# The first channel layer of two more batches by seven block products, and 134 shifted entries in a planned instruction order

## The chip, the cores and the metric

The kernel runs on one core of one Trainium2 chip. The metric is the device time of that core in microseconds (us). Before the change it is 276.57 us, the median of three runs (276.26 to 276.59). The profile comes from one further execution, which took 276.21 us. The engines are named as in the profile: PE is the matrix engine, PEld its weight load, DVE the vector engine, ACT the scalar engine, POOL and SP the two that mostly issue transfers. A "pass" is one matmul instruction: it streams its moving columns past 128x128 loaded weights.

## The reference

Eight batches go through windowed attention with a linear bias, and the result through two mixing layers:

```python
# attention: B=8, H=8 heads, S=576 positions, D=64
scores = scale * q @ k.T ; scores = where(0 <= i-j < 128, scores - slope[h]*|i-j|, -1e9)
x = (softmax(scores) @ v) with the heads side by side        # 8 x 576 x 512
# mixer
h  = relu(x.T @ w_tok1) @ w_tok2                              # 576 -> 256 -> 576, along positions
u  = x + h.T
h2 = relu(u @ w_ch1) @ w_ch2                                  # 512 -> 1536 -> 512, along channels
out = u + h2
```

Inputs and output are float32. The kernel works in bf16 with float32 sums.

## The kernel before

**Batches and stages.** Batches are numbered from 0, so the fourth and the sixth are 3 and 5. Each has four blocks of 128 positions; two batches share one more block for the 64 positions left over of each (the "tail" block). A batch passes through `side` (attention scores L770 and L816, exponentials on ACT L785, masks on DVE L795, values L858, reciprocals L871 and normalisation L874 or, on ACT, L880; then the token mix L905, L915, and L948, L944, whose sums with x go to `ub` by DVE L966), and then through `main`. `main` of batch b is written together with `side` of batch b+1, so the two share the engines. Between them, for batches 3 to 7, `ub` is turned into `uT` by transfers that SP issues (L974, one for each block); SP also issues the turns of q and k (L722) and most stores of the output.

**First channel layer.** `main` computes relu(u @ w_ch1) into `r2`: 12 chunks of 128 hidden rows for 512 positions. A plain chunk (`chunk`, L1460) is four passes of 512 columns into one PSUM bank, and one relu, on ACT (L1466) or DVE (L1467). The tail block has its own passes (L1503, L1548).

**Seven products.** `unit` replaces four chunks. It regards hidden rows, channels and positions as halved, and forms the 2x2 block product from seven block products instead of eight, each of four passes of 256 columns (L1360). They need the differences of the halves of `uT` (`halves`, L1323: four DVE subtractions a batch, stored in `tt`) and of the weights (`WS`, made once at L688). Three banks y, z, w are used: products 1, 6, 7 and 4 add up in y, product 2 is in z, products 5 and 3 in w. Three intermediate sums are copied out as e1, e5, e2 (`keep`, L1375, ACT or DVE, into the five float32 buffers `raw`/`ob` that also hold outputs). Three sums are completed on DVE (`join`, L1384: bank plus copy, to bf16), each followed by a relu in place (L1386 on DVE or L1388 on ACT); the fourth quarter is relued straight from y (L1411, ACT). Product 6 waits for the copy of 1, product 7 for the copy of 6, product 4 for the join of 7. They are declared in the order of `UORDER`, 1, 5, 2, 6, 3, 7, 4. The list `UNITS` says for each batch how many of its three groups of four chunks go this way; before, only the last batch has any.

**Second channel layer.** It already takes seven products in all batches (`second`, L1637, 84 passes of 256 columns), with DVE sums of `r2` (L1485) ahead of it and DVE additions behind it (L1608).

**Who sets the order.** The order of every engine's instructions is computed while the program is built. `Plan.op` records each operation with its engine, a cost in ns, a rank, a not-before (`after`), its predecessors and its buffers; `Plan.run` plays the operations through these costs and picks, for each engine, the candidate that could start first, the lower rank among those that are equal. An operation with `other` may go to either DVE or ACT. PSUM banks and other buffers are handed out in the same pass. The outcome is a fixed program: each engine takes its instructions strictly in the order written, and waits where an operand or a buffer is not ready. Units may use all eight banks only once the last score operation of the batch beside them is placed (`gated`); until then they have four, as the value products and the token mix have.

Of the kernel before, what the change touches and what calls it, by code (L numbers as in the profile page):

```python
# [71 lines left out]
class Plan:  # L72
# [59 lines left out]

    def run(self):
        ops = self.ops
        dice = [random.Random(x) for x in SEEDS]
        for o in ops:
            if SEEDS[o.part]:
# [241 lines left out]
GROUPS = (((0, 1, 2, 3), 250),)  # L379
UORDER = (1, 5, 2, 6, 3, 7, 4)  # L380
UNIT_RANK = 0
UNIT_LATE = False
SECOND_LATE = False
GATE = True
BANKS = 8
ALIKE = 0
UNITS = [0, 0, 0, 0, 0, 0, 0, 3]
FILL = 60000.0
START = 4300.0
LATE = (1500.0, 2790.0)  # L390
# [26 lines left out]
def kernel(  # L417
# [244 lines left out]
    def weight_sums():  # L662
        lo, hi = slice(0, HN), slice(HN, DM)
        for g in range(2):
            a, z = slice(3 * g, 3 * g + 3), slice(HK + 3 * g, HK + 3 * g + 3)
            got = []
            for i, x, y in ((0, WC2[:, a, hi], WC2[:, a, lo]), (1, WC2[:, z, hi], WT[:, 0, a, :]),
                            (2, WC2[:, z, hi], WC2[:, a, hi]), (3, WC2[:, z, lo], WT[:, 1, a, :])):
                def go(i=i, x=x, y=y, a=a):
                    dve_.tensor_tensor(out=WT[:, i, a, :], in0=x, in1=y, op=ALU.subtract)  # L670
                needs = [lc2[3 * g]] if i == 0 else [lc2[3 * g], lc2[HK + 3 * g]] + ([got[i // 2]] if i % 2 else [])
                got.append(plan.op("DVE", 154 + 3 * HN / 1.92, go, RANKT + i, needs=needs))
            lt.append(got)
# [3 lines left out]
    def hidden_sums():  # L677
        for u in range(NHT // 4):
            up, dn = slice(2 * u * P, 2 * (u + 1) * P), slice(DCH // 2 + 2 * u * P, DCH // 2 + 2 * (u + 1) * P)
            x, y = slice(0, NCB // 2), slice(NCB // 2, NCB)  # L680
            own = slice(2 * u * P, 2 * (u + 1) * P)
            got = []
            for i, f, a, z in ((0, ALU.add, WC1[:, x, dn], WC1[:, y, dn]),
                               (1, ALU.subtract, WS[:, 0, :, own], WC1[:, x, up]),
                               (3, ALU.subtract, WC1[:, y, up], WS[:, 1, :, own]),
                               (2, ALU.subtract, WC1[:, x, up], WC1[:, x, dn])):
                def go(i=i, f=f, a=a, z=z, own=own):
                    dve_.tensor_tensor(out=WS[:, i, :, own], in0=a, in1=z, op=f)  # L688
                needs = [lc1[x] for x in (2 * u, 2 * u + 1, 6 + 2 * u, 7 + 2 * u)]
                needs += [got[-1]] if i in (1, 3) else []  # L690
                got.append(plan.op("DVE", 154 + 2 * 2 * P / 1.92, go, RANKS + i, needs=needs, after=SUMS_AT))
            ls.append({1: got[0], 2: got[1], 4: got[2], 3: got[3]})
# [12 lines left out]
    weight_sums()  # L705
    if any(UNITS):
        hidden_sums()
# [621 lines left out]
    def unit(b, u, rank, uT, tt, r2):  # L1329
# [24 lines left out]
        def product(m, bk, more=(), new=True):  # L1354
            l, r, ws, ts = L[m]

            def go():
                for c in range(2):
                    for cb in range(2):
# [6 lines left out]
                         **({"makes": bk} if new else {"adds": bk}))  # L1366
            if UNIT_LATE and new:
                marks["wait"].append(op)
            return rk

        def half_of(x):
            return x().rearrange("p (c n) -> p c n", c=2)

        def keep(e, bk, rk):
            return plan.op("ACT", 600, lambda: act_.copy(out=e()[:, :], in_=bk()[:, :]), rk + UNIT_RANK, makes=e, uses=[bk],  # L1375
                           other=("DVE", 690, lambda: dve_.tensor_copy(out=e()[:, :], in_=bk()[:, :])))

        def mark(op, rows):
            for t in range(rows.start, rows.stop):
                r2.parts.setdefault(t, []).append(op)  # L1380

        def join(e, bk, rows, cols, rk):
            o = lambda: r2()[:, rows, cols]
            add = plan.op("DVE", 690, lambda: dve_.tensor_tensor(out=o(), in0=half_of(bk), in1=half_of(e), op=ALU.add),  # L1384
                          rk + UNIT_RANK, uses=[bk, e], part=(r2, ("sum", rows.start, cols.start)))
            mark(plan.op("DVE", RELU, lambda: dve_.tensor_scalar(out=o(), in0=o(), scalar1=0.0, scalar2=None, op0=ALU.max),  # L1386
# [47 lines left out]
    def main(b, rank):  # L1434
# [76 lines left out]

        if not UNITS[b]:
            turn_ = [0, 1, 2, 6, 7, 8, 3, 4, 5, 9, 10, 11] if quick else list(range(NHT))
# [6 lines left out]
        else:  # L1520
            tt = halves(b, rank, uT)
            for u in range(NHT // 4):
                if u >= NHT // 4 - UNITS[b]:
                    rk = unit(b, u, rank, uT, tt, r2)
# [205 lines left out]
```

## Time and profile before

| what | value |
|---|---|
| median of three runs | 276.57 us |
| profiled execution | 276.21 us |
| its span, first to last instruction | 274.2 us |
| PE busy | 267.9 us (98%) |
| DVE busy | 209.4 us (76%) |
| ACT busy | 136.9 us (50%) |
| granted PE clock | 1.000 |

The time of the execution is 2.0 us longer than the span of its instructions. Batch 3's first layer starts at 121.1 us of the span and its last channel pass ends near 156.1; for batch 5 these are 183.5 and 218.5; the units of the last batch run from 245 to 261 us. A matmul's listed duration (273 or 379 ns) holds its time in the pipeline; what a pass costs in a row of passes is read from the chain of work, as the time of a piece over its count.

### The profile page before, as it was taken

To read this page: it belongs to the slowest core of one execution; us is meant where nothing else is said; L and a number is where in the kernel's file an instruction comes from. 1 tells how busy PE (TensorE), PEld (TensorE's weight loads), DVE (VectorE), ACT (ScalarE), POOL (GpSimd) and SP (SyncE) were. 2 spreads that over 40 slices of the span, in tenths; PEclk is the share of its full clock that TensorE was granted. 3 is DMA by queue.
4 is the path that set the end of the run, shared out by engine and by line. 5 is a ranking of instruction groups with operands and counts; after the bars stand their busy time and mean duration, and the time that the engine had idled before them with its cause. 6 is when DMAs were issued, how large, how long until landed. Compare 5 with 4: busy or idle time off the path is not lost.

```text
span 274.2 us, 7149 instructions
## 1 busy us (share of the span) xinstructions
PE 267.9 (98%) x2896; PEld 182.2 (66%) x2896; DVE 209.4 (76%) x482; ACT 136.9 (50%) x221; POOL 114.3 (42%) x146
## 2 busy tenths in 40 slices
PE   8989999999999999999999999999999999999994
PEld 5767566676686656585658656486658655489983
DVE  7987699977997479675968469684969469697972
ACT  6963795326871396207930097206940087205500
POOL 8979796830496009600890009700850410022000
PEclk9999999999999999999999999999999999999999
DMA  8999999999999999979999939989995810143014
GB/s 201 178 175 181 166 159 182 155 157 197 157 118 141 199 161 103 154 119 199 192 151 136 211 127 89 150 119 214 181 142 91 229 42 2 28 108 116 2 41 151
DMA packets 160336, 38.57 MB, mean 141 GB/s; under 512 B 146544, under 2 KB 159472, under 8 KB 160304
## 3 DMA queue, kind: packets, MB, share of 16 engines
q0 software_dynamic: 109968, 19.64, 90.2%
q1 hardware_dynamic: 49104, 17.70, 34.3%
q10 hardware_dynamic: 1232, 0.79, 1.0%
q8 instruction: 22, 0.36, 0.6%
q14 instruction: 10, 0.08, 0.1%
HBM read 35.85 MB, written 9.44 MB: 165 GB/s over the span
## 4 chain that ended last, share of the span: by engine, by line
PE 92%; DMA 4%; ACT 1%; issue 1%; POOL 0%; DVE 0%; POOLq 0%
PE ps L1637 27%; PE ps L1460 26%; PE ps L858 6%; PE ps L770 5%; PE ps L905 4%; PE ps L948 4%; PE ps L1503 4%; PE ps L1548 4%; PE ps L1360 3%; DMA W<-in_moe_w_tok_dram 2%; DMA v<-in_v_dram 2%; PE ps L1446 1%; PE ps L733 1%; PE ps L915 1%; PE ps L944 1%; PE ps L983 1%
## 5 line engine op out<-in xcount | busy, mean ns | idle before, releaser
L1466 ACT ACTIVATE r<-ps 128x512 bf16<-128x512 f32 x73 | 43.3, 600 | 76.1 <-PE ps L1460 68.9
L1460 PE MATMUL ps<-uT,WC 128*128 128x512 bf16 x324 | 78.7, 379 | 0.0
L579 POOL DMA_DIRECT2D v<-in_v_dram x36 | 30.6, 850 | 84.4 <-PE ps L858 81.8
L785 ACT ACTIVATE pe<-ps 128x1024 bf16<-128x1024 f32 (+1 forms) x56 | 50.9, 962 | 0.9 <-PE ps L770 0.8
L1460 PEld LDWEIGHTS <-WC 128*128 128x128 bf16 x324 | 29.1, 98 | 29.9 <-issue 1.1
L1637 PEld LDWEIGHTS <-r 128*128 128x128 bf16 x384 | 36.7, 98 | 6.7 <-issue 0.9
L579 POOL DMA_DIRECT2D qk<-in_q_dram x35 | 30.3, 869 | 4.0 <-DMA qkT<-qk 2.0
L579 POOL DMA_DIRECT2D qk<-in_k_dram x35 | 30.3, 871 | 3.7 <-DMA qk<-in_k_dram 1.3
L795 DVE TENSOR_TENSOR pe<-pe,mask 128x1024 bf16<-128x1024 bf16 (+1 forms) x48 | 30.4, 650 | 1.5 <-ACT pe L785 1.3
L1637 PEld LDWEIGHTS <-s 128*128 128x128 bf16 x288 | 27.7, 98 | 4.7 <-issue 1.0
L1637 PE MATMUL ps<-WC,r 128*128 128x256 bf16 x192 | 25.3, 273 | 0.0
L874 DVE TENSOR_TENSOR xb<-ps,rt 128x256 bf16<-128x256 f32 (+1 forms) x60 | 24.5, 419 | 0.7
L966 DVE TENSOR_TENSOR ub<-ps,xb 128x512 bf16<-128x512 f32 x32 | 19.8, 681 | 5.2 <-PE ps L948 5.2
L1637 PE MATMUL ps<-WT,r 128*128 128x256 bf16 x192 | 23.8, 273 | 0.0
L1637 PE MATMUL ps<-WT,s 128*128 128x256 bf16 x192 | 23.6, 273 | 0.0
L1608 DVE TENSOR_TENSOR raw<-ps,ub 128x512 f32<-128x512 f32 x27 | 18.2, 681 | 6.7 <-PE ps L1637 6.6
L858 PE MATMUL ps<-v,pe 128*128 128x65 bf16 (+1 forms) x480 | 21.9, 195 | 0.0
L858 PEld LDWEIGHTS <-pe 128*128 128x128 bf16 (+1 forms) x480 | 18.4, 99 | 5.2 <-DVE pe L795 1.1
L1620 POOL DMA_DIRECT2D out_dram<-raw x6 | 4.3, 718 | 37.0 <-DVE raw L1608 37.0
L770 PEld LDWEIGHTS <-qkT 64*128 64x128 bf16 x448 | 11.9, 94 | 8.9 <-issue 7.4
L1608 DVE TENSOR_TENSOR raw<-ps,raw 128x512 f32<-128x512 f32 x19 | 13.0, 688 | 5.9 <-PE ps L1637 5.9
L1467 DVE TENSOR_SCALAR r<-ps 128x512 bf16<-128x512 f32 x11 | 7.5, 686 | 11.1 <-PE ps L1460 8.9
(142 smaller groups left out, 400.0 us busy)
## 6 DMA issues: line engine op xcount, KB each, us to landing
out_dram<-raw SPq DMA_DIRECT2D x21, 256.0 KB, 3.5
qk<-in_q_dram POOLq DMA_DIRECT2D x30, 128.0 KB, 6.3
qk<-in_k_dram POOLq DMA_DIRECT2D x30, 128.0 KB, 6.1
v<-in_v_dram POOLq DMA_DIRECT2D x28, 128.0 KB, 6.1
WC<-in_moe_w_ch_dram POOLq DMA_DIRECT2D x8, 384.0 KB, 7.0
out_dram<-raw POOLq DMA_DIRECT2D x6, 256.0 KB, 3.4
v<-in_v_dram POOLq DMA_DIRECT2D x16, 64.0 KB, 4.8
out_dram<-ob SPq DMA_DIRECT2D x3, 256.0 KB, 2.7
```

Source lines behind the costliest of these rows:

```text
L579: nc.gpsimd.dma_start(out=to()[p0 : p0 + n, :, :], in_=rows(src, b, s0, n))
L770: pe_.matmul(wide(e)[:, i, kind, a:z], lhsT=ts[kb]()[e * D : (e + 1) * D, NHP + i, :], rhs=ts[blk]()[e * D : (e + 1) * D, i, a:z], start=T ...
L785: act_.activation(out=pb()[:, e, :, lo:, c0:c1_], in_=wide(e)[:, :, lo:, c0:c1_], func=ACT.Exp, scale=scale)
L795: dve_.tensor_tensor(out=o, in0=o, in1=heads(mk, es), op=ALU.mult)
L858: pe_.matmul(view()[a:z, at, i, :], lhsT=pb()[:, e, i, kind, a:z], rhs=vb()[:, h, 0 : D + 1], start=m == 0, stop=m == len(mms) - 1, skip_g ...
L874: dve_.tensor_tensor(out=x4(), in0=view()[r0:r1_, :, :, 0:D], in1=rt()[r0:r1_, 0:n, :, :].broadcast_to([r1_ - r0, n, 4, D]), op=ALU.mult)
L905: pe_.matmul(t1[j]()[:, :], lhsT=W1[:, blk % NC, j * P : (j + 1) * P], rhs=xb()[:, blk, :], start=c == 0, stop=False)
L966: plan.op("DVE", 690, lambda blk=blk, ht=ht, hs=hs: dve_.tensor_tensor(out=ub()[:, blk, :], in0=ht()[:, hs], in1=xb()[:, blk, :], op=ALU.a ...
L1460: pe_.matmul(ct()[:, :], lhsT=WC1[:, cb, t * P : (t + 1) * P], rhs=uT()[:, cb, :], start=cb == 0, stop=cb == NCB - 1)
L1466: plan.op("ACT", 600, lambda t=t, ct=ct: act_.activation(out=r2()[:, t, :], in_=ct()[:, :], func=ACT.Relu), rk, part=(r2, t), uses=[ct], o ...
L1608: dve_.tensor_tensor(out=v, in0=bk().rearrange("p (c n) -> p c n", c=2), in1=src, op=ALU.add)
L1637: pe_.matmul(bk()[:, c * HN : (c + 1) * HN], lhsT=l(t, c), rhs=w(t), start=first, stop=g == 1 and t == HK - 1, skip_group_check=True)
```

## The change

Two things change together. Batches 3 and 5 get `UNITS` 3, so all twelve chunks of the first channel layer of each become three units. And before the planning starts, 134 operations, named by their number in the order of declaration, get a number added to their rank and, most of them, a later not-before (in ns of the planner's clock). The functions `halves`, `unit` and `chunk` themselves are as they were.

```diff
     def run(self):
         ops = self.ops
+        for item in NUDGES.split():
+            n, rank, after = item.split(":")
+            ops[int(n)].rank += float(rank)
+            ops[int(n)].after = max(ops[int(n)].after, float(after))
...
+NUDGES = ("94:12660:106875 616:7571:109297 618:4019:0 621:-1414:103243 629:-8944:115592 635:4216:0 642:11590:0 "
...
+          "1382:694:254562 1388:1747:0 1398:4906:262159 1421:12247:262982 ")
...
-UNITS = [0, 0, 0, 0, 0, 0, 0, 3]
+UNITS = [0, 0, 0, 3, 0, 3, 0, 3]
```

In the program that comes out, PE has 168 passes of 256 columns at L1360 more and 96 passes of 512 columns at L1460 less; its other passes are the same in number, and so are the 92 places behind the first 28 us of passes where it changes between whole-array and half-array passes. On DVE there are 8 more subtractions (L1323), 18 more joins (L1384), 11 more relus in place (L1386) and one more copy (L1376), and 2 less chunk relus (L1467), 2 less normalisations (L874) and 4 less copies of 64 rows (L898). On ACT there are 17 more copies (L1375), 7 more relus in place (L1388), 6 more relus from the bank (L1411), two normalisations more (8 instructions at L880) and 4 more copies of 64 rows (L900), and 22 less chunk relus (L1466). POOL and SP issue the same transfers in another order. PE's order is the same up to about 91 us of passes, ahead of batch 3's token mix; from there the passes of the second layer and of the side work stand in smaller pieces between each other than before. All line numbers here and below are those of the kernel before.

More of the change, by code (lines that the diff above doesn't have):

```diff
@@ L381 @@
 UNIT_RANK = 0
+NUDGES = ("94:12660:106875 616:7571:109297 618:4019:0 621:-1414:103243 629:-8944:115592 635:4216:0 642:11590:0 "
+          "644:-4232:128802 651:15153:119629 669:-1407:103608 676:-4837:0 683:-755:105459 685:-1934:105499 693:-14786:0 "
+          "706:-20285:107153 710:8058:0 728:2035:0 731:0:118331 737:19107:123898 747:-1255:129898 750:-29231:133352 "
+          "752:10280:131265 753:10825:0 757:-11969:129250 761:30009:131162 763:-4902:130888 765:11844:134943 "
+          "766:9498:138150 769:14121:135329 776:-3993:125106 778:22085:0 779:5333:138621 780:17313:136913 782:3889:0 "
+          "793:4049:0 809:6520:152268 810:4802:137007 816:8492:157025 835:33287:124325 843:-8130:125662 857:-7911:124420 "
+          "859:32920:132589 861:-24489:131883 862:15088:133394 869:-3419:126643 877:2715:0 879:-18088:134693 893:-31339:0 "
+          "894:-4758:134773 908:4589:151484 912:5178:0 925:-1570:166030 926:-8590:0 939:8864:174432 941:0:178068 "
+          "954:7362:0 964:-2098:0 970:-4835:0 983:-3979:162202 985:-5355:161279 990:-6199:165475 991:942:0 994:4002:0 "
+          "996:-321:164112 999:-1597:156677 1011:-4404:169514 1036:1664:177289 1043:1174:181265 1045:873:185505 "
+          "1062:5667:189154 1065:1967:0 1069:1868:191667 1071:-10162:188222 1073:3645:194114 1074:8884:0 1076:40042:0 "
+          "1079:12013:0 1080:-4452:195024 1081:-15700:197245 1085:-3084:202479 1090:-11770:198747 1092:-1173:0 "
+          "1103:2124:204537 1110:8985:212154 1124:4777:0 1153:1184:0 1156:-13748:189170 1161:1615:191431 1162:666:0 "
+          "1170:2959:192895 1172:-1945:195991 1173:-8567:194582 1174:2151:201011 1179:-729:0 1180:1254:199015 1182:1397:0 "
+          "1184:9130:197876 1185:6661:0 1188:3423:198395 1192:4992:0 1195:-958:203140 1197:4131:0 1198:3077:203297 "
+          "1201:-277:204124 1206:4609:200272 1211:-15286:207270 1212:4795:210875 1229:1131:225023 1242:3425:221060 "
+          "1256:2496:0 1265:-11760:232292 1266:6725:0 1267:3396:245277 1288:1474:0 1293:-3479:224027 1302:2750:0 "
+          "1305:3543:0 1311:-634:0 1314:-4090:230229 1323:4190:233417 1326:-3293:0 1329:-4136:0 1340:2634:0 "
+          "1341:6380:241194 1344:-7486:0 1346:5891:0 1351:7172:244441 1357:-4688:0 1369:3059:252380 1380:-18658:250883 "
+          "1382:694:254562 1388:1747:0 1398:4906:262159 1421:12247:262982 ")
 UNIT_LATE = False
```

## The prediction

> **What bounds the kernel now.** I read the page first: busy times, slices and the chain that ended last.
>
> ```profile
> span 274.2 us, 7149 instructions
> PE 267.9 (98%) x2896; PEld 182.2 (66%) x2896; DVE 209.4 (76%) x482; ACT 136.9 (50%) x221; POOL 114.3 (42%) x146
> ...
> PE   8989999999999999999999999999999999999994
> DVE  7987699977997479675968469684969469697972
> PEclk9999999999999999999999999999999999999999
> PE 92%; DMA 4%; ACT 1%; issue 1%; POOL 0%; DVE 0%; POOLq 0%
> ```
>
> PE is on 92% of the chain, its clock is full throughout, and its slices are full from the second on. A full slice doesn't say that passes follow each other without a hole, so the next view is that of the waits, for PE alone; these are its longest two of four.
>
> ```profile
> PE ps L1695 <- DVE zero L530: 1.0, 1, 1.0
> PE ps L1201 <- DMA W<-in_moe_w_tok_dram: 0.6, 1, 0.6
> ```
>
> All four lie in the opening; asked for 30 to 270 us alone, the view has no line. From there PE runs through, and the time is the sum of its passes. So the third view is the chain in order of time, for the price of a pass in a row.
>
> ```profile
> 123.40 1.73 PE ps L1460 x8
> ...
> 249.08 0.89 PE ps L1503 x16
> 249.98 3.06 PE ps L1360 x28
> 253.03 0.89 PE ps L1503 x16
> 253.93 3.06 PE ps L1360 x28
> ```
>
> A pass of 512 columns costs 1.73/8 = 0.216 us, one of 256 columns 3.06/28 = 0.109 us. The pieces of the last batch's units follow each other without a gap (249.98 + 3.06 = 253.04).
>
> **The passes.** A group of four chunks is 16 x 0.216 = 3.46 us; a unit is 28 passes, 3.06 us. Six groups change: 6 x (3.46 - 3.06) = 2.40 us less PE work. The changes between whole-array and half-array passes are as many as before (92), so the finer interleaving costs nothing there. This gain is certain as work; the question is what of it PE loses again by waiting.
>
> **The vector work.** Rows of the groups, by form (mean ns behind the comma):
>
> ```profile
> L1466 ACT ACTIVATE r<-ps 128x512 bf16<-128x512 f32 x73 | 43.3, 600 | 76.1 <-PE ps L1460 68.9 <-DVE xt L898 3.3 <-PE ps L1446 1.7
> L966 DVE TENSOR_TENSOR ub<-ps,xb 128x512 bf16<-128x512 f32 x32 | 19.8, 681 | 5.2 <-PE ps L948 5.2
> L874 DVE TENSOR_TENSOR xb<-ps,rt 128x256 bf16<-128x256 f32 x58 | 23.7, 419 | 0.7
> L1467 DVE TENSOR_SCALAR r<-ps 128x512 bf16<-128x512 f32 x11 | 7.5, 686 | 11.1 <-PE ps L1460 8.9 <-ACT pe L785 1.7 <-PE ps L1446 0.4
> L1384 DVE TENSOR_TENSOR r<-ps,raw 128x512 bf16<-128x512 f32 x8 | 5.5, 690 | 1.2 <-PE ps L1360 1.0
> L1375 ACT COPY raw<-ps 128x512 f32<-128x512 f32 x8 | 4.5, 586 | 11.4 <-PE ps L1360 11.4
> L880 ACT ACTIVATE xb<-ps,rt 128x64 bf16<-128x64 f32 x16 | 3.8, 335 | 0.0
> L1386 DVE TENSOR_SCALAR r<-r 128x512 bf16<-128x512 bf16 x8 | 2.4, 294 | 0.3
> L898 DVE COPY xt<-xb 64x512 bf16<-64x512 bf16 x5 | 2.1, 416 | 0.2
> L900 ACT COPY xt<-xb 64x512 bf16<-64x512 bf16 x2 | 1.2, 617 | 4.0 <-DVE xb L874 4.0
> L1323 DVE TENSOR_TENSOR tt<-uT,tt 128x512 bf16<-128x512 bf16 x2 | 0.8, 416 | 0.0
> L1388 ACT ACTIVATE r<-r 128x512 bf16<-128x512 bf16 x1 | 0.6, 622 | 0.0
> ```
>
> DVE gains 8 x 0.416 (subtractions) + 18 x 0.690 (joins) + 11 x 0.294 (relus) + 0.690 (a copy, as a join) = 19.7 us, and loses 2 x 0.686 + 2 x 0.419 + 4 x 0.416 = 3.9: 15.8 us more, 7.9 a batch. ACT gains 17 x 0.586 + 7 x 0.622 + 6 x 0.600 + 8 x 0.335 + 4 x 0.617 = 23.1 and loses 22 x 0.600 = 13.2: 9.9 us more, 5.0 a batch. Where this must fit are the two stretches from a batch's first chunk to its last channel pass:
>
> ```profile
> 121.10:156.10 35.00, 35.00 (x368) 23.34 (x366) 23.36 (x50) 15.80 (x23) 13.68 (x16) 1.00 1.58 180
> 183.50:218.50 35.00, 35.00 (x368) 23.36 (x366) 23.52 (x50) 15.80 (x23) 12.14 (x15) 1.00 1.23 167
> ```
>
> The columns are length, then busy PE, PEld, DVE, ACT, POOL. The stretch shrinks to 33.8 us; DVE goes from 23.4 to 31.3 (93%), ACT from 15.8 to 20.8 (62%). Listed durations overlap: the 32 additions at L966 take 19.8 us together, not 32 x 0.681 = 21.8, so 9% less is nearer, some 30.6 us. I cost the added DVE and ACT work at nothing: PE's passes cover it. If the cover goes, each us by which DVE runs behind is one on PE.
>
> **Waits inside a unit.** Product 7 waits for the copy of 6 (0.586 on ACT), product 4 for the join of 7 (0.690 on DVE, in its order among masks and normalisations). In the new order, at the closest place (batch 5, second unit), 8 passes of 256 columns and 8 value passes lie between 7 and 4, 8 x 0.109 + 0.2 = 1.1 us, which covers a join by 0.4. One mask (0.68) ahead of it in DVE's queue would use that up; behind the join stand the masks and normalisations of the next batch's attention, and PE's value passes wait for those. Bounds: nothing, as in the last batch's units (no gap in the chain above); at most a bare join for each of the six units, 6 x 0.69 = 4.1 us. The order has other passes at all six places, so I take a value near the lower end, 0.3 us. The five float32 buffers shared with the outputs, and the banks (three of four held by a unit until the last scores are placed), are in this figure: a late join also frees its bank late.
>
> **What is late next: the turns of `u`.** The new order puts the first chunk of batches 4 and 6 closer behind the token mix that makes their `u`, because second-layer passes of batches 3 and 5 moved ahead of the mix. SP's turns lie between. The chain, PE's and SP's rows for batch 4, and SP's for batch 6:
>
> ```profile
> 142.57 1.73 PE ps L948 x8
> ...
> 156.13 1.03 PE L1460 MATMUL ps<-uT,WC 128*128 128x512 bf16 x4
> ...
> L974 SPq DMA_TRANSPOSE uT<-ub x4: 1199/1210/1789, 143.8 to 147.7; - x4
> DMA to landing us min/median/max: 4.9/6.2/7.5
> ...
> L974 SPq DMA_TRANSPOSE uT<-ub x4: 1190/1216/1217, 206.2 to 210.1; - x4
> DMA to landing us min/median/max: 2.3/2.3/2.4
> ```
>
> Batch 4: `u` is complete on PE at 144.3, the last turn lands at 147.7 + 4.9 = 152.6 (8.3 us later), the chunk starts at 156.1, 3.5 us spare. New: behind the last L948 pass come 4 passes L1360, 12 of L1548 (512 columns) and 48 of L1637, 0.4 + 2.6 + 5.2 = 8.2 us, and then the chunk. Nothing is spare if the turns land as late as here; if as in batch 6 (2.3), 0.68 (addition) + 1.2 (turn) + 2.3 = 4.2 us do, and 4 are spare. One store moves between the third and fourth turn on SP, and waits for a DVE addition (0.7). Batch 6 gets 0.65 + 2.6 + 0.65 + 1.3 = 5.2 us against the same 4.2, again with a DVE addition or two ahead: just enough. Bounds: nothing to 2 x 0.7 us; I take 0.3 for both. The loads on POOL are the same in number and come in another order; before they had slack, and I cost that at nothing, at worst the 5.2 us by which turns land apart (7.5 against 2.3) in one batch.
>
> **The nudges** add no work; they only set the order costed here. The last batch's units now run 80 passes in a row, with two tail pieces ahead of them instead of between. Its 9 joins (6.2 us) and 5 relus (1.5) must fit into 8.7 us of passes; the piece of 28 above, with as dense joins, had no gap. Zero, bounds -0.2 to +0.7 (one join).
>
> **Sum.** -2.4 + 0.3 + 0.3 = -1.8 us. The profiled execution (276.21 us: span 274.2 and 2.0 around it, which doesn't change) would become 274.4. It was 0.36 under the median of the runs shown; from that median, 276.57, I get 274.8.
>
> **A rule weighed.** The rows above give a pass 0.216 and 0.109 us, in proportion to its columns. The Trainium skill, page "TensorE: Matmul & The Clock Gate", section "Back-to-back issue gap", says that in streams of weight load and matmul the spacing is set by both, and gives about 81 ns a pass at 128 columns and 131 at 512. By its figures a group of chunks is 16 x 131 ns = 2.10 us and a unit at least 28 x 81 ns = 2.27, so the change would add at least 1.0 us (an estimate from that page). The trace disagrees with the 131 ns.
>
> **The rivals.**
> 1. *DVE lags.* 93% by listed durations leaves 2.5 us a stretch, and a join behind a burst of masks and normalisations keeps product 4 and a bank waiting. For it: three dependent products in one bank. Against: the cover of 1.1 us, the 9% overlap, ACT at 62%. Price: half to one and a half us more a batch beside my 0.6: 275.4 to 277.
> 2. *The turns come late, and it is slower.* Place: first chunk of batch 4 or 6, behind SP's turns, which wait behind POOL's loads on the transfer engines. Landings vary by 5.2 us. Above 2.4 us of waiting, nothing is gained; as batch 4 has no spare by its own rows, a landing 3.1 us later than now gives 276.57 - 2.4 + 3.1 = 277.3. Against: its loads had all been issued by then, and a later turn finds a shorter queue.
> 3. *Weight loads bind.* Twice as many weights are loaded for a column:
>
> ```profile
> L1360 PEld LDWEIGHTS <-WS 128*128 128x128 bf16 x48 | 4.6, 98 | 0.5
> ```
>
> 98 ns fits under 109 by 11 ns. Were it exposed for the 72 passes more, 7.1 us: 281.3. Against: these same passes already ran at 0.109 in the last batch. This is also the mechanism of the rule above.
> 4. *Nothing changes*, because something other than PE sets the end, 276.5. Against: no wait of PE over 240 us.
>
> **How the numbers follow.** 0.2% (0.55 us) is about what a measurement tells from no change. Forecast (274.0 to 275.4): 0.63; more than the forecast, with no waits at all, under 274.0: 0.04; rival 1: 0.17, of which 0.11 still faster than 276.0, 0.03 within, 0.03 slower; rival 2: 0.11, slower; rival 3: 0.01; rival 4: 0.04, of which 0.03 within and 0.01 slower. Faster 0.78, same 0.06, slower 0.16. The range leaves out the top two tenths: 273.9 to 276.5.
>
> **What would show it.** Right: in the profile after, PE busy near 265.5, L1360 252 times, the chain's pieces at 0.109 us a pass, DVE near 225 us, and no line of PE over half a us. Step by step: a wait of PE at L1360 or L858 for DVE r or pe is rival 1; at L1460 for a transfer to uT near 153 or 216 us it is rival 2; a piece of L1360 above 0.109 a pass is rival 3. The prediction is wrong if those waits sum to more than 2 us.

## The result, and the profile after

The changed kernel takes 275.17 us (median of seven runs, 274.46 to 275.99). Its ratio to the kernel before is 0.9942, with an interval of 0.9925 to 0.9959, so it is 1.6 us faster (1.1 to 2.1). Two more series gave 0.9936 (0.9913 to 0.9959) and 0.9926 (0.9896 to 0.9956).

From here on, line numbers are those of the kernel after the change, except in rows of the kernel before; every line named is 24 higher than before: L1360 is now L1384, L1460 L1484, L1637 L1661, L1384 L1408, L858 L882, L770 L794, L1323 L1347, L966 L990, L974 L998, L1608 L1632. The profiled execution took 275.34 us. From its page, busy times, slices and the chain that ended last:

```profile
span 273.6 us, 7290 instructions
PE 264.2 (97%) x2941; PEld 189.0 (69%) x2968; DVE 222.5 (81%) x512; ACT 144.7 (53%) x241; POOL 114.6 (42%) x146
...
PE   7989999999999999999999899999999999999994
DVE  7887699977997488789999369798998749876982
...
PE 84%; DMA 5%; DVE 3%; POOL 3%; issue 2%; ACT 1%; SPq 0%; DVEq 0%; POOLq 0%
```

DVE has risen from 209.4 to 222.5 us, and PE holds a smaller share of the chain (84% in place of 92): there are now places where the chain leaves it. PE's records are 27 short of its weight loads (2941 against 2968), so PE's busy time, read from matmuls, is a little low. The chain in order of time shows the price of a narrow pass in a longer row than before, 4.80/44 = 0.109 us:

```profile
247.84 4.80 PE ps L1384 x44
```

Who PE waited for, between 30 and 270 us, where it had waited for nobody:

```profile
PE ps L1484 <- DMA uT<-ub: 0.7, 1, 0.7
PE ps L1384 <- DMA uT<-ub: 0.2, 1, 0.2
PE ps L929 <- issue: 0.2, 1, 0.2
PE ps L1484 <- issue: 0.2, 1, 0.2
```

Two waits are for turns of `u`: at 154.1 us, ahead of batch 4's first chunk, and at 121.0, ahead of batch 3's first unit. By the distance between the passes on both sides they cost 0.90 and 0.34 us (a little of a wait is not put down to it in the view). No line names DVE or ACT. Short waits can't be seen here, though: a narrow pass is listed with 0.273 us and followed by the next after 0.109, and the view leaves out gaps under 0.15 us, so a wait of less than some 0.3 us goes unnamed. The load of the two stretches (length, then busy PE, PEld, DVE, ACT, POOL):

```profile
121.30:155.00 33.70, 32.60 (x386) 25.55 (x391) 30.23 (x66) 18.65 (x29) 13.64 (x16) 1.00 1.68 168
182.60:216.90 34.30, 34.14 (x404) 27.06 (x405) 31.20 (x68) 18.48 (x30) 10.33 (x13) 1.00 1.12 142
```

DVE is busy for 90 and 91% of them.

A single profile is not quite the median run. Runs of one kernel lie up to 3.9 us apart (275.80 to 279.70 for the kernel before in the third series), and the profiled pair differs by 276.21 - 275.34 = 0.87 us, half of what the medians do. So below, waits are taken as shown only where a second profile or the medians agree.

Part of this scatter lies ahead of the change. PE's order is that of the kernel before up to a row of passes that starts near 99 us. In the kernel before, in the profile above, and in two more profiles of the changed kernel (`after_again` and `after_third` below), this row is (x7 where a record is missing):

```profile
98.97 1.89 PE L1460 MATMUL ps<-uT,WC 128*128 128x512 bf16 x8
98.93 1.89 PE L1484 MATMUL ps<-uT,WC 128*128 128x512 bf16 x7
100.35 1.89 PE L1484 MATMUL ps<-uT,WC 128*128 128x512 bf16 x7
99.17 1.89 PE L1484 MATMUL ps<-uT,WC 128*128 128x512 bf16 x8
```

So the same opening differs by up to 1.4 us from one execution to the next. It is fairer to compare from this row on. The last row of passes, in the same four profiles:

```profile
269.23 1.32 PE ps L1548 x12
268.57 1.32 PE ps L1572 x12
269.07 1.32 PE ps L1572 x12
267.96 1.32 PE ps L1572 x12
```

From the start of the one to the end of the other, PE takes 171.58 us before, and 170.96, 170.04 and 170.12 after: 0.6, 1.5 and 1.5 us less. A second, small part of the gain is outside the span. A run of the changed kernel takes 1.7 to 1.9 us more than its span; for the kernel before, run beside it, the median is 2.0. No run shows where these 0.2 us come from.

### The profile page after: what moved, and what is told of

The parts are those of the page before. It is cut to its first block, busy times and chain, and to the rows that moved or that the text cites. A ratio compares the mean times of both kernels' runs of the same rounds, so it can differ in the third digit from the quotient of the medians.

```text
span 273.6 us, 7290 instructions
## 1 busy us (share of the span) xinstructions
PE 264.2 (97%) x2941; PEld 189.0 (69%) x2968; DVE 222.5 (81%) x512; ACT 144.7 (53%) x241; POOL 114.6 (42%) x146
## 4 chain that ended last, share of the span: by engine, by line
PE 84%; DMA 5%; DVE 3%; POOL 3%; issue 2%; ACT 1%; SPq 0%; DVEq 0%; POOLq 0%
PE ps L1661 22%; PE ps L1484 18%; PE ps L1384 10%; PE ps L882 6%; PE ps L794 5%; PE ps L929 4%; PE ps L1527 4%; PE ps L972 4%; DMA uT<-ub 3%; PE ps L1572 3%; DMA W<-in_moe_w_tok_dram 2%; DVE ub L990 2%; POOL v L612 1%; POOL qk L619 1%; PE ps L757 1%
## 5 line engine op out<-in xcount | busy, mean ns | idle before, releaser
L603 POOL DMA_DIRECT2D v<-in_v_dram x36 | 30.6, 852 | 88.1 <-PE ps L882 85.5
L1484 PE MATMUL ps<-uT,WC 128*128 128x512 bf16 x214 | 53.6, 379 | 1.4 <-DMA uT<-ub 0.7
L1490 ACT ACTIVATE r<-ps 128x512 bf16<-128x512 f32 x51 | 29.6, 601 | 35.7 <-PE ps L1484 33.7
L1661 PEld LDWEIGHTS <-r 128*128 128x128 bf16 x384 | 36.6, 98 | 7.0 <-issue 0.9
L1484 PEld LDWEIGHTS <-WC 128*128 128x128 bf16 x228 | 20.2, 97 | 21.4 <-issue 1.4
L819 DVE TENSOR_TENSOR pe<-pe,mask 128x1024 bf16<-128x1024 bf16 (+1 forms) x48 | 30.2, 650 | 3.4 <-ACT pe L809 3.2
L1661 PEld LDWEIGHTS <-s 128*128 128x128 bf16 x288 | 27.6, 98 | 6.0 <-issue 1.1
L1661 PE MATMUL ps<-WC,r 128*128 128x256 bf16 x192 | 25.4, 273 | 0.0
L882 PEld LDWEIGHTS <-pe 128*128 128x128 bf16 (+1 forms) x480 | 19.7, 99 | 7.3 <-DVE pe L819 0.8
L1661 PE MATMUL ps<-WT,s 128*128 128x256 bf16 x192 | 24.4, 273 | 0.0
L898 DVE TENSOR_TENSOR xb<-ps,rt 128x256 bf16<-128x256 f32 (+1 forms) x58 | 23.5, 417 | 0.6
L1661 PE MATMUL ps<-WT,r 128*128 128x256 bf16 x192 | 23.7, 273 | 0.1
L882 PE MATMUL ps<-v,pe 128*128 128x65 bf16 (+1 forms) x480 | 23.2, 194 | 0.2
L990 DVE TENSOR_TENSOR ub<-ps,xb 128x512 bf16<-128x512 f32 x32 | 20.3, 682 | 2.6 <-PE ps L972 2.5
L1399 ACT COPY raw<-ps 128x512 f32<-128x512 f32 x23 | 13.1, 594 | 17.1 <-PE ps L1384 16.9
L1632 DVE TENSOR_TENSOR raw<-ps,ub 128x512 f32<-128x512 f32 x27 | 18.4, 684 | 3.3 <-PE ps L1661 3.3
L1408 DVE TENSOR_TENSOR r<-ps,raw 128x512 bf16<-128x512 f32 x23 | 15.6, 683 | 2.7 <-PE ps L1384 2.0
L1632 DVE TENSOR_TENSOR raw<-ps,raw 128x512 f32<-128x512 f32 x20 | 13.7, 688 | 4.4 <-PE ps L1661 4.3
```

Source lines behind the costliest of these rows:

```text
L603: nc.gpsimd.dma_start(out=to()[p0 : p0 + n, :, :], in_=rows(src, b, s0, n))
L819: dve_.tensor_tensor(out=o, in0=o, in1=heads(mk, es), op=ALU.mult)
L882: pe_.matmul(view()[a:z, at, i, :], lhsT=pb()[:, e, i, kind, a:z], rhs=vb()[:, h, 0 : D + 1], start=m == 0, stop=m == len(mms) - 1, skip_g ...
L898: dve_.tensor_tensor(out=x4(), in0=view()[r0:r1_, :, :, 0:D], in1=rt()[r0:r1_, 0:n, :, :].broadcast_to([r1_ - r0, n, 4, D]), op=ALU.mult)
L990: plan.op("DVE", 690, lambda blk=blk, ht=ht, hs=hs: dve_.tensor_tensor(out=ub()[:, blk, :], in0=ht()[:, hs], in1=xb()[:, blk, :], op=ALU.a ...
L1484: pe_.matmul(ct()[:, :], lhsT=WC1[:, cb, t * P : (t + 1) * P], rhs=uT()[:, cb, :], start=cb == 0, stop=cb == NCB - 1)
```

## The experiments

**The late turns.** First question: are the two waits for `u` what keeps the gain from 2.4 us? The order of SP suggested so for batch 4: the shift "908:4589:151484" puts the turn of its first block last, with a store ahead of it.

```profile
148.03 1.22 SPq L998 DMA_TRANSPOSE uT<-ub  x1
150.45 0.37 SPq L1644 DMA_DIRECT2D out_dram<-raw  x1
150.87 1.74 SPq L998 DMA_TRANSPOSE uT<-ub  x1
```

SP stood still from 149.25 to 150.45, until DVE's addition for that store was done, with the turn behind it. The changed kernel ran again, beside a kernel with the turn moved ahead:

> The changed kernel as it is, for comparison with the three below on the same chip. Both theories: ratio to the kernel before 0.994, within 0.0925 to 0.996 of it as measured, some 1.6 us less. In its profile the theory of the late turns expects PE's wait at the first chunk of batch 4 (near 154 us, for the last transfer into uT) again at 0.5 to 1 us.

Measured: 274.65 us, ratio 0.9936 (0.9913 to 0.9959); the view has one wait for `u`, 0.4 us at the first L1384 (0.55 by the distance between passes), and none at batch 4.

```diff
# turn_first: in Plan.emit, ahead of the sorting by t0 (908 is the turn, 813 the store)
+        self.ops[908].t0 = self.ops[813].t0 - 1.0
```

> On SP alone, the fourth turn of batch 4's u stands ahead of the store of batch 3's output, not behind it; every other engine has the same instructions. Theory of the late turns: SP no longer stands still from 149.3 to 150.4 us, the turn lands about 0.7 us earlier (154.2 in place of 154.9), PE's wait near 154 us falls from 0.9 to at most 0.2 us, and the whole takes 0.5 to 0.9 us less than the changed kernel. Rival, that vector work sets the pace behind it: no gain, within 0.2 us of the changed kernel, since the next wait takes the place of this one.

Measured: 274.80 us, 0.9929 (0.9907 to 0.9951). There is no wait at batch 4, as there was none in the kernel beside it either, and nothing is gained. Nor did the turn land earlier: SP issued it at 150.8 us, 1.7 us ahead of the kernel beside it (152.5), and in both it landed near 155.0, after 4.2 and 2.6 us. The wait of 0.9 us belongs to some runs, not to the kernel as such. The profile of `turn_first` has instead a wait of 1.1 us at 77 us for a turn of q and k, at a place where the order is that of the kernel before: single turns come late now here, now there.

```diff
# no_loads
-        work = [(o.t0, o.n, o.emit) for o in self.ops]
+        work = [(o.t0, o.n, o.emit) for o in self.ops if not (94 <= o.n <= 103 or 110 <= o.n <= 119)]
```

> Leaves out 20 loads of q, k and v that POOL issues at 106 to 115 and 135 to 145 us, so the attention of the last batches uses old data; all else is the same. Theory of the late turns, that these loads stand ahead of the turns of batches 3 and 4 on the transfer engines: landings fall to 2 to 3 us, the waits at 121 (0.34 us) and 154 us (0.9) go, 1.0 to 1.5 us less than the changed kernel. Rival, that the loads are no hindrance and the turns are late by SP's order alone: the first landings stay at 4 us and more, less than 0.3 us gained.

Measured: 274.52 us, 0.9923 (0.9895 to 0.9951). In this kernel's trace, the turns of batch 3 and the time to their landing:

```profile
L998 SPq DMA_TRANSPOSE uT<-ub x4: 1212/1216/1258, 112.7 to 116.6; - x4
DMA to landing us min/median/max: 2.3/2.4/2.4
```

In the changed kernel the same four, issued at the same time, took longer:

```profile
L998 SPq DMA_TRANSPOSE uT<-ub x4: 1207/1221/1258, 112.6 to 116.5; - x4
DMA to landing us min/median/max: 3.8/4.8/4.8
```

Without POOL's loads the turns land in half the time and PE's wait at batch 3 is gone (both waits for `uT` have left its view). That part of the theory holds: the turns are late because of the loads. But the whole gains 0.1 us over the changed kernel beside it, not 1.0 to 1.5; the intervals allow some tenths. The span does get shorter by 0.55 us (medians 272.85 and 272.30), as much as the wait that has gone from the profile beside it; the time outside the span gets longer by 0.4 (from 1.8 to 2.2 us), and no run shows why.

The order on SP explains why batch 3 waits at all. Product 1 reads the first half of the positions, the batch's first two blocks, and the shift "728:2035:0" raises the rank of the second block's turn, which puts it last of four. The third try moves it back to second place, and the turn of `turn_first` too:

```diff
# turn_order (728, 729: turns of batch 3's second and third block)
+        self.ops[908].t0 = self.ops[813].t0 - 1.0; self.ops[728].t0 = self.ops[729].t0 - 1.0
```

> The changed kernel with two turns moved ahead on SP: that of batch 3's second block from fourth to second place, and that of batch 4's last block ahead of the store. Product 1 reads the first two blocks alone, so PE's wait at the first L1384 near 121 us (0.34, 0.55 and 0.76 us in three profiles) goes to under 0.1 us, and none is left near 154: 0.3 to 0.9 us less than the changed kernel. Rival, the loads decide whatever the order: the first turns land as late as the last did, wait unchanged, within 0.2 us.

> The changed kernel once more, to compare with turn_order on the same chip: ratio 0.993 to 0.995 to the kernel before, a wait of 0.3 to 0.8 us at the first L1384 near 121 us, and at the first chunk of batch 4 either none or up to 1 us.

Measured: 274.65 us, 0.9921 (0.9894 to 0.9948), against 274.84 for the changed kernel beside it, 0.9926 (0.9896 to 0.9956). In the trace of `turn_order` the view of PE's waits between 30 and 272 us is empty; that of the changed kernel beside it has one line:

```profile
PE ps L1384 <- DMA uT<-ub: 0.3, 1, 0.3
```

So the wait at batch 3 comes from the place of one turn behind the loads, and goes with it. The turns land no sooner (4.1 to 5.2 us), but the late one is no longer the one that product 1 reads. What this is worth, 0.4 us by the distance between passes in the kernel beside it and 0.2 by the medians, is less than these runs can tell apart. It is the best order found, but not shown to be faster.

**The vector work.** Second question: how much room does DVE have?

```diff
# relu_twice; relu_none has "lambda: None" there
-            mark(plan.op("DVE", RELU, lambda: dve_.tensor_scalar(out=o(), in0=o(), scalar1=0.0, scalar2=None, op0=ALU.max),
+            mark(plan.op("DVE", RELU, lambda: [dve_.tensor_scalar(out=o(), in0=o(), scalar1=0.0, scalar2=None, op0=ALU.max) for _ in range(2)],
```

> Each of the 19 relus in place on DVE stands twice in a row (same result), some 0.21 us of DVE time each without overlap, 4 us in all, about two thirds of it in the two changed batches. Theory of the late turns: DVE has room, 0 to 0.6 us more than the changed kernel. Rival, DVE sets the pace: 2 to 4 us more.

Measured: 278.86 us, 1.0072 (1.0047 to 1.0097), 4.2 us more than the changed kernel beside it by the medians, 3.8 by the ratios. The page of this kernel:

```profile
span 277.4 us, 7308 instructions
...
PE 266.4 (96%) x2941; PEld 188.8 (68%) x2968; DVE 227.5 (82%) x531; ACT 145.0 (52%) x241; POOL 114.6 (41%) x146
```

DVE is busy for 5.0 us more, and some three quarters of that is paid. PE's waits in the same trace, between 30 and 272 us:

```profile
PE ps L882 <- DVE r L1408: 0.4, 1, 0.4
...
PE ps L1661 <- DVE raw L1632: 0.3, 1, 0.3
...
PE ps L882 <- DVE xb L898: 0.2, 1, 0.2
```

The group of the value passes (busy time and mean ns of one, then idle time before them and what ended it):

```profile
L882 PE MATMUL ps<-v,pe 128*128 128x65 bf16 (+1 forms) x480 | 23.2, 194 | 1.2 <-DVE r L1408 0.4 <-DVE xb L898 0.2
```

In the changed kernel that group's idle time is 0.2 us in place of 1.2. The value passes wait for the bank that a join still holds, or a normalisation. No wait is long; they are many. What they wait for stands behind the doubled relus in DVE's order, while few waits are for the relus themselves; so by this trace it is DVE's lateness that costs, and not a longer step from join to second layer.

> Leaves out the 19 relus in place on DVE (so those hidden values stay without relu), same order otherwise: some 4 us of DVE time less. Theory that DVE has just no room left in the changed batches (doubling these relus cost 4 us): 0.3 to 1.0 us less than the changed kernel, mostly where PE waited between 120 and 145 and between 190 and 205 us. Rival, that DVE has ample room and the doubled relu hurt in another way, as a longer step in the chain from join to second layer: less than 0.2 us gained.

Measured: 274.22 us, 0.9909 (0.9888 to 0.9930), against 274.65 and 0.9936 for the changed kernel, which ran in another series: 0.4 to 0.7 us less, with intervals that overlap. DVE fell to 28.93 and 29.89 us in the two stretches, 86 and 87%. Together the two runs say that the changed kernel stands at the edge: less DVE work brings little, as PE hardly waits for it; more costs some 0.8 us for each us that it adds.

**The two parts of the change, one by one.**

```diff
# no_nudges
-NUDGES = ("94:12660:106875 ...
+NUDGES = ""
```

> Units in batches 3, 5 and 7 as changed, the 134 shifts left out, so the planner's own order stands. Theory that the shifts keep the waits small, by putting second-layer and tail passes between a unit's dependent products: 1 to 2.5 us more than the changed kernel (275.8 to 277.2), with waits of PE at the passes of L1384 and at the first L1661 behind the token mix. Rival, that the saved passes carry the gain whatever the order: within 0.4 us of the changed kernel.

Measured: 277.17 us, 1.0033 (1.0005 to 1.0062): a little slower than before, and 2.0 to 2.5 us above the changed kernel by the medians, 2.5 to 3.0 by the ratios (some 0.2 of it outside the span, where this kernel spends 2.0 us). PE's waits in its trace, between 30 and 272 us:

```profile
PE ps L1661 <- DVE raw L1632: 2.3, 2, 1.9
PE ps L882 <- ACT r2t L1532: 0.5, 2, 0.2
PE ps L882 <- DVE r L1408: 0.4, 2, 0.2
PE ps L1527 <- DVE r L1408: 0.4, 2, 0.2
```

The last three come in pairs, one in each changed batch. By the distances between passes they cost 0.36, 0.36 and 0.40 us, so 1.1 us a batch: value and tail passes wait for banks that joins and tail relus still hold. That is nearly all that a batch's units save (1.2 us). The Trainium skill, page "Perfetto Trace Analysis", section "Optimization Strategy", calls such bubbles, the same gap repeated on the engine that should be full, a possible sign that there isn't enough SBUF or PSUM for the next tile. The trace agrees as far as it goes: the named releasers are the operations that empty banks; no run here has more banks.

> Units in batch 3 (and 7, as before), no shifts. If a batch's units save 1.2 us of passes and lose half of it by waits in the planner's own order, 0.4 to 0.9 us less than the kernel before; if the order eats all of it, within 0.3 us of the kernel before.

```diff
# only3, without the shifts; units135, also without them, has [0, 3, 0, 3, 0, 3, 0, 3]
-UNITS = [0, 0, 0, 3, 0, 3, 0, 3]
+UNITS = [0, 0, 0, 3, 0, 0, 0, 3]
```

Measured: 277.48 us, 1.0018 (0.9993 to 1.0042). Nothing is gained: the order eats all of it. Its trace has the three small waits of batch 3 again.

The first line of `no_nudges`, 1.9 us near 121.7 us, seemed to be the larger part. There DVE had begun on the subtractions of `tt`, which wait for the turns of `u`, and an addition that PE waited for stood behind them in DVE's order. In the changed kernel the shifts have it ahead of them.

```diff
# sums_behind, on no_nudges: the first three subtractions behind the addition, in batches 3 and 5
+        for n, m in ((732, 647), (734, 647), (733, 647), (1044, 959), (1046, 959), (1045, 959)): self.ops[n].t0 = self.ops[m].t0 + 1.0 + n % 4;
```

> The kernel without shifts, in which DVE's order alone is altered at two places: the first three subtractions of batch 3's and batch 5's halves, which wait for the turns of u, stand behind the addition of the second layer (L1632) that stood behind them. Theory that most of what the shifts bring is this order on DVE: PE's waits of 2.0 us at 121.6 and 0.6 at 186 us (for DVE raw) fall to at most 0.5 in all, and the whole takes 1.8 to 2.6 us less than without shifts, near the changed kernel. Rival, that it is the interleaving of PE's passes that counts: less than 1 us gained, the wait comes again at the next dependent pass.

Measured: 277.86 us, 1.0042 (1.0011 to 1.0073): no gain. This trace has neither of the two waits, but new ones, the longest in batch 5, and the same three pairs as above:

```profile
PE ps L1384 <- ACT ob L1399: 0.7, 1, 0.7
...
PE ps L794 <- ACT pe L809: 0.4, 1, 0.4
...
```

So the theory that DVE's order at this place is most of what the shifts bring has fallen. The 1.9 us belong to some executions: three of the twelve lie 1.9 to 3.5 us above the median of 277.17, the profiled one (279.06 us) among them, and in it the last turn of batch 3 took 4.4 us to land. In `only3`, with the same order there, it took 2.3, and the line stands at 0.2. What stays in all three traces are the three small waits a batch, 2.2 us for two batches, and the changed kernel has none of them in its view. So the shifts' worth seems to lie in the interleaving of PE's passes; this is read from the traces, as no run changes that interleaving alone.

```diff
# shifts_only: UNITS as before, and the 105 shifts whose operation exists there too, renumbered
-UNITS = [0, 0, 0, 3, 0, 3, 0, 3]
+UNITS = [0, 0, 0, 0, 0, 0, 0, 3]
```

> The other part alone: plain chunks in batches 3 and 5 as before, and those 105 of the 134 shifts whose operation exists there too, under their numbers in that program. Theory that the shifts are worth 2.3 us only with the units, since without them PE waits for nothing that an order could fill: within 0.5 us of the kernel before, or somewhat slower. Rival, that the shifts are a better order by themselves and the units add little: 1 us or more less than the kernel before.

Measured: 279.98 us, 1.0113 (1.0081 to 1.0146), 3.1 us more than before. PE's waits:

```profile
PE ps L1484 <- DMA uT<-ub: 1.6, 1, 1.6
PE ps L882 <- DVE xb L898: 0.7, 1, 0.7
...
```

Here the first chunk of batch 5 stands too close behind the turns. 29 of the shifts are missing, so this isn't the shifts' worth as such; it shows that they fit this one set of operations. By ratios, units alone cost 0.3%, shifts alone 1.1%, both save 0.6 to 0.7%.

**One batch more.**

> Units in batches 1, 3, 5 and 7, no shifts: 1.2 us of passes less than without batch 1's, and 8 us more of DVE and ACT work around 53 to 93 us, where DVE is 88% busy by the page's slices. Theory that DVE's room decides: no gain from batch 1 beyond the run without shifts, or a loss to 1 us. Rival, passes decide: 0.8 to 1.2 us less than the run without shifts.

Measured: 279.01 us, 1.0090 (1.0062 to 1.0117), 1.8 us above the run without batch 1's units. The waits that this adds, between 50 and 95 us:

```profile
PE ps L1661 <- DVE r L1408: 1.0, 1, 1.0
PE ps L1661 <- DVE raw L1632: 0.9, 1, 0.9
PE ps L1384 <- ACT raw L1399: 0.7, 1, 0.7
PE ps L1527 <- DVE xb L898: 0.3, 1, 0.3
```

Passes saved are worth nothing where DVE and ACT can't empty the banks in time: 1.2 us saved, 2.9 us waited.

## Why the prediction was right, and where it wasn't

- *The passes, -2.4 us.* The rows bear it out: 0.109 us a pass again, in rows up to 44 long, and PE's order has no more places of change between array modes. All of it is there: where no turn is late, in `turn_order`, PE needs 2.1 us less than before from the row near 99 us to its end (100.30 to 269.77 us of the span, 169.47 in place of 171.58), and three short waits make up the rest. What the kernel gains, 1.6 us, is two thirds of it.
- *The rule weighed.* With 72 more weight loads the passes kept 0.109 us, and the kernel got faster, not slower by 1.0 us. Rival 3, and the 131 ns at 512 columns of the Trainium skill, page "TensorE: Matmul & The Clock Gate", section "Back-to-back issue gap", have no support here.
- *DVE and ACT load.* Forecast 30.6 us of DVE in a stretch of 33.8; measured 30.2 of 33.7 and 31.2 of 34.3. ACT was forecast at 20.8 and is 18.6. Over the whole kernel DVE rose by 13.1 us and ACT by 7.8, where the sums of listed durations gave 15.8 and 9.9, as they leave out that instructions overlap; the rest of what ACT lacks here falls outside the two stretches.
- *"I cost the added DVE and ACT work at nothing: PE's passes cover it".* This came true, but the reason was better than the working. At 91 to 93% of a stretch I took the cover to be a matter of total load. `no_nudges` has the same kind of load (29.9 and 30.5 us in 35) and loses 1.1 us a batch. The order decides, and the second sentence, that each us by which DVE runs behind is one on PE, is borne out by `relu_twice` at some 0.8 us for each us.
- *Waits inside a unit, 0.3 us.* Right in size. In five profiles, three of the changed kernel and two that differ only on SP, no wait of PE for DVE or ACT is in the view after 30 us. The distances between passes show what is too short for it: holes of 0.05 to 0.2 us at L1384, L882 and L1661, for copies, joins, normalisations and additions, together 0.3 to 0.5 us in the changed kernel and 0.27 in `turn_order`. The cover of 1.1 us between products 7 and 4 was the right thing to look at.
- *The turns, 0.3 us.* The mechanism was right: batch 4, a store between the third and fourth turn, behind a DVE addition. The place was half right. Batch 4 waited in one of three profiles of the changed kernel, batch 6 in none; batch 3, which I didn't name, waited in all of the five but the one that moves its turn (0.3 to 0.8 us). I had compared distances of whole batches and missed that a turn of batch 3 had moved to the last place, and that product 1 reads only the first two blocks. The term measured 1.2, 0.55 and 0.4 us in the three profiles, not 0.3.
- *"The nudges add no work".* True, and the step that says least: the 134 shifts are worth 2.0 to 2.5 us by the medians, more than the gain; two of them put the late turns where they are. The prediction had this in it only because it read the order that came out, and did not price the two parts apart.
- *"2.0 around it, which doesn't change".* It changed: 1.8 us outside the span, in place of 2.0. That the sum of -1.8 came near 1.6 is in part luck, as this 0.2 us offsets turns that cost more than forecast.
- *The signs.* No line of PE over half a us was one of them: the first profile has 0.7 us at the first chunk of batch 4, the other two have none so long. PE's busy time (264.2 us, with 27 records missing) and DVE's (222.5) came out a little below the 265.5 and 225 named.
- *The rivals.* Rival 1, DVE behind and banks held, isn't what the changed kernel does, but it is what the units do without the shifts, in one batch or three. Rival 2 is there in its small form, some tenths. Rival 4, that something else sets the end, is out.

The difference between 2.4 us and the gain is thus mostly accounted for. In the three profiles of the changed kernel, late turns (1.2, 0.55, 0.4 us) and short holes (0.5, 0.3, 0.45) leave 0.6, 1.5 and 1.5 of the 2.4 us, as measured from the row near 99 us on. Left open: what sets the time outside the span, and why the turns land so differently from one execution to the next.

## What to carry to other kernels

Where one engine is full, count what a change takes from it, but then read whether the engines that empty its buffers keep up in the order given: at 90% load the same work was a gain of 1.6 us in one order and a loss in another. To find out how much room a covering engine has, double a harmless instruction on it; the answer is sharper than its busy share. And when transfers are reordered, ask of each consumer which of them it really reads, and whether that one has become the last.

## What the runs showed of the hardware that I had not expected

Batch 3's turns, issued by SP, took 3.8 to 4.8 us to land behind POOL's loads, and 2.3 to 2.4 us with the loads left out. Whether PE waited at the first product hung on this and on their order: in `turn_order` they took 4.1 to 5.2 us, and PE didn't wait. In the one pair of profiles that allows the comparison, a turn issued 1.7 us earlier (`turn_first`) landed no earlier. And the turns' lateness varies between executions of the same program: 0.9 us of waiting at one place in one profile, none there in the next two. In `turn_first` there were 1.1 us at another place, where the order is that of the kernel before.
